# Swapped spectrum halves copied into the dead rows of k in a long convolution fused with an FFN

## The chip, the core and the metric

The kernel runs on one core of a Trainium2 chip. Its engines work side by side, each through its own list of instructions in order: TensorE (PE) for matrix products and transposes, VectorE (DVE), ScalarE (ACT), GpSimd (POOL), and SyncE (SP), which here only issues DMA transfers. They meet through semaphores. The metric is the device time of one execution in microseconds (us); the table below gives the median of the runs.

## The reference

All inputs are bf16; the sequence has 2048 rows of 640 channels. The same normalized input goes into a gated long convolution and into a feed-forward network, and the two results are multiplied:

```python
xn = _layernorm(A_q, axis=-1)
# A: four-tap shift of k, product with v, causal convolution of length 2048 by FFT, times xn
k_shift = sum over t of k_pad[:, t:t + S, :] * shift_k[:, ks - 1 - t]
kv = k_shift * v
y = irfft(rfft(kv, 2 * S) * rfft(ssm_k, 2 * S))[:, :S] + kv * ssm_D
s = xn * y
# B: two layers, 640 -> 1728 -> 640
g = silu(gelu(xn @ w1 + b1) @ w2 + b2)
return A_q + s * g
```

## The kernel before

Everything is on chip but three scratch arrays in DRAM, scrK, scrU and scrC, through which the rows of a transform are regrouped between its two halves. The transforms are matrix products with matrices of sines (WA, WB for the first half; F2m, I1a, I1b in `mats`; GA, GB for the last half). The FFN runs in four chunks of 512 rows.

The order of the work is written out by hand: PLAN is a list of 906 steps, and a loop at the end calls them one after the other. A step is a kind, a number and, for evictions from PSUM, the engine (`.a` ScalarE, `.d` VectorE). The order of the steps of one engine in PLAN is the order of its queue, SP's and POOL's included. Semaphores are set from the data that steps share. The kinds that matter here:

- `P`, `X`, `A`, `B`, `K`, `V`, `C`: loads of parameters, x, w1, w2, k, v and the filter; `pt`, `pb`: transpose of the parameters and the cast of b1 from PSUM, which every `he` needs; `s`, `ss`, `sm`: the small sine matrices; `w`, `ws`: the large ones; `em`, `ee`: the fourth tap's weights.
- `h0` to `h55` and `he`: first FFN layer (five matmuls each) and its gelu on ScalarE, 14 for a chunk. `g0` to `g31`, `ge`, `gm`: second layer (14 matmuls), silu on ScalarE, product on VectorE. `tt`, `te`: transposes of x for a chunk and their copies out; `ls`, `lv`, `lr`, `ln`: the layer norm.
- `cv0` to `cv63`: the shift of k and the product with v on VectorE, eight steps for each of eight pairs of rows. `kt`, `kc`, `kf`, `ke`, `ks`: transpose of the filter, its copy, first transform, cast, store to scrK. `uf`, `ue`, `us`: the same for u = k_shift * v, to scrU.
- `fl`, `ff`, `fe`: load of a pair from scrK, second transform, cast into the spectrum Khat[:, g] (32 blocks g).
- `ml`: load of a pair of u blocks from scrU, after all sixteen `us`. `mu`: their second transform. `mk`: two DMAs that copy a pair of Khat's blocks with their upper and lower 64 partitions exchanged (the "swap"). `mp`: the complex product of u's block, Khat's block and its swap on VectorE. `mc`, `me`, `ms`: first half of the inverse, cast, store to scrC.
- `yl`, `y`, `yt`, `yo`, `ys`: load from scrC, last half of the inverse, gate, sum with x, store. `ga`, `gs`: the same for the last chunk of rows. `q`: load of x for the sum.

Buffers on the way: PSUM has three large tiles ("big") and two small ones ("ffn") that its pools hand out in turn. Khat has 32 spectrum rows and eight more (NR), which the class Ring hands out as four pairs in turn: first to casts of kf and uf, and then to `mk`. The 19 rows of k, the tile kh, are dead once the last `cv` has read them; another Ring hands them out as nine pairs: first to `ml`, then to `yl`.

```python
    pools["ring"] = Ring(Khat, NG, NR // 2)
    pools["line"] = Ring(kh, 0, (NJ + 3) // 2)
```

So a swap waits until the products of the swap four before it are done, and what stands behind it in SP's queue waits too.

Of the kernel before, what the change touches and what calls it, by code (L numbers as in the profile page):

```python
# [50 lines left out]
uf31 gm11 ge12 uf30 ue30.a ue31.d us15 ff23 fe23.d gm12 uf23 ue23.a us11 gm10 tt14 te14.d uf29 uf28 ue28.d
ue29.a us14 mk0 ml0 ml1 mk1 mk2 mk3 ml2 ml3 ml5 ml4 ff31 fe31.a tt13 te13.a tt10 te10.d it0 ie0.d ff27 fe27.d
ff25 fe25.d g13 ge13 gm13 g14 ge14 gm14 ff29 fe29.d ln14 ff28 fe28.a ff24 fe24.d g15 ge15 gm15 ff21 fe21.a tt11
te11.d ff22 fe22.a mu0 mp0 ff26 fe26.a ml7 h28 he28 mu2 mp2 ml10 ml8 mu1 mp1 mk4 mc0 me0.a h29 he29 ff30 fe30.a
mu3 mp3 mk5 ml12 h30 he30 ml11 mc2 me2.a mu4 mp4 mc1 me1.a ms0 mu5 mp5 mk6 h31 he31 ml6 ff20 fe20.a mc3 me3.a
ms1 ln15 mu6 mp6 mc4 me4.a mu7 mp7 mk7 ml9 h32 he32 mu8 mp8 mc5 me5.a ms2 mc6 me6.a mu11 mp11 mc7 me7.a ms3 mu10
mp10 h33 he33 mu9 mp9 mk8 mk9 mc8 me8.a mc10 me10.a mu12 mp12 mu13 mp13 mk10 mc11 me11.a ms5 ml14 h34 he34 ml15
mc12 me12.a it1 ie1.d mc13 me13.a ms6 mu15 mp15 h35 he35 mu14 mp14 mk11 ml13 mc9 me9.a ms4 mu18 mp18 h36 he36
mc14 me14.a mu17 mp17 h37 he37 mu16 mp16 mk12 mc15 me15.a mu20 mp20 h38 he38 mu19 mp19 mk13 mc18 me18.a h39 he39
mu21 mp21 mk14 mc16 me16.a tt17 mc19 me19.a ms9 mc17 me17.a ms8 mu23 mp23 mc20 me20.a mu22 mp22 mk15 h40 he40  # L60
# [14 lines left out]
def kernel(  # L75
# [31 lines left out]
    ps_ffn = ctx.enter_context(tc.tile_pool(name="ps_ffn", bufs=2, space=bass.MemoryType.PSUM))  # L107
    ps_big = ctx.enter_context(tc.tile_pool(name="ps_big", bufs=3, space=bass.MemoryType.PSUM))
# [21 lines left out]
    def big(name):  # L130
        return ps_big.tile([P, 2, 512], F32, tag="big", name=name)
# [9 lines left out]
    Khat = wts.tile([P, NG + NR, D], BF16, name="Khat")  # L141
# [20 lines left out]
    kh = ep.tile([P, NJ + 3, D], BF16, name="kh")  # L162
# [141 lines left out]
    def w_exp_matmuls(j):  # L304
        ps = big("psw")
# [4 lines left out]
        return ps  # L310
# [12 lines left out]
    def big_of(key, bf=False):  # L323
        return take(key, ps_big, [P, 1024] if bf else [P, 2, 512], BF16 if bf else F32, "big")

    def ffn_of(key, bf=False):
        return take(key, ps_ffn, [P, 1024] if bf else [P, 512], BF16 if bf else F32, "ffn")

    def row_of(key):
        return take(key, ep, [P, D], BF16, "row", NROW)  # L330

    def pair_of(key):
        return take(key, ep, [P, 2, D], BF16, "pair", NPAIR)

    def quad_of(key):
        return take(key, ep, [P, CH, D], BF16, "quad", 2)
# [46 lines left out]
    def ffn1_out(i):  # L383
        ft = i % FT
        M = min(P, F - ft * P)
        nc.scalar.activation(out=hT[0:M, ft, :], in_=live["h", i][0:M, :], func=ACT.Gelu_apprx_tanh,  # L386
                             bias=b1_f[0:M, ft:ft + 1], scale=1.0)
# [14 lines left out]
    def ffn2_silu(i):  # L402
        sl = take(("sl", i), ffnp, [P, HALF], BF16, "sl", 2)
        nc.scalar.activation(out=sl[:], in_=live["g", i][:, 0:HALF], func=ACT.Silu)  # L404
# [305 lines left out]
```

## Time and profile before

| what | us |
|---|---|
| three runs: lowest, median, highest | 231.13, 231.67, 232.67 |
| the profiled execution, its own time | 232.81 |
| its span (first to last instruction) | 231.0 |
| mean granted TensorE clock in it | 0.984 |

In the lines below, a group of instructions is given as line, engine, operation, output and inputs by the program's names with buffer numbers left out (so kh, Khat or uc), count, then busy time and mean duration in ns. In a timeline the first number is the start in us from the start of the span, the second the length; in brackets stands how long the engine had been idle, and what ended that. "SPq" rows are issues of DMAs by SyncE. A matmul's record is 0.16 longer than the pace of such matmuls, since neighbours overlap. "DMA to landing" is from the issue to the arrival.

What follows shows where each engine is in the program:

| stretch of the span | work |
|---|---|
| 0 to 16 | loads, layer norm of the first chunk, taps |
| 16 to 57 | first chunk of the FFN, filter's first transform, `cv` on VectorE |
| 57 to 119 | second chunk, first transforms of filter and u, second of the filter |
| 119 to 172 | third chunk's `h`, `mu`, `mp`, `mc` |
| 172 to 231 | rest of the third chunk, last inverse, fourth chunk, outputs |

### The profile page before, as it was taken

The page shows a single profiled execution, that of the slowest core. Times are in us where ns is not written, and L with a number is a line of the kernel's source. Part 1 is how long each engine was busy: PE and PEld are TensorE (multiplying, and loading weights), DVE is VectorE, ACT ScalarE, POOL GpSimd, SP SyncE. Part 2 cuts the span into 40 slices and gives each one's busy share as a digit, 9 for nine tenths or more (in the row PEclk, how much of TensorE's full clock was granted, in tenths as well). Part 3 has the DMA queues.
Part 4 walks back from the last instruction along what each step waited for, and adds up shares of the span by engine and source line. Part 5 has one row for each costly group of instructions (what it writes and reads, how often), then busy time and mean ns, then how long its engine had stood idle before and what let it go on. Part 6 is the DMA issues. An engine that isn't in the chain of part 4 may idle for free.

```text
span 231.0 us, 3921 instructions
## 1 busy us (share of the span) xinstructions
PE 211.6 (92%) x1420; PEld 131.7 (57%) x1420; DVE 184.1 (80%) x315; ACT 149.6 (65%) x232; POOL 43.1 (19%) x75
## 2 busy tenths in 40 slices
PE   7859999899999899979999965999999999999993
PEld 4524456677555556646765532556677765457772
DVE  7799999889989999999779885699998115444892
ACT  3934687998988999898468742567782244562111
POOL 8100020042232344120200220212222000100010
PEclk9988999999999999999999997999999999999999
DMA  7999995654844479599779999877943695379323
GB/s 219 349 380 355 409 413 206 191 209 174 305 191 188 179 236 381 176 309 337 266 215 294 303 353 295 257 231 188 270 156 131 207 340 200 150 218 367 124 89 114
DMA packets 25209, 57.61 MB, mean 249 GB/s; under 512 B 2854, under 2 KB 14055, under 8 KB 25190
## 3 DMA queue, kind: packets, MB, share of 16 engines
q1 hardware_dynamic: 20726, 39.66, 52.6%
q0 software_dynamic: 4320, 17.70, 20.5%
q8 instruction: 11, 0.18, 0.3%
q14 instruction: 8, 0.07, 0.1%
q10 hardware_dynamic: 144, 0.01, 0.0%
HBM read 33.76 MB, written 18.35 MB: 226 GB/s over the span
## 4 chain that ended last, share of the span: by engine, by line
PE 65%; ACT 12%; DMA 9%; DVE 8%; issue 3%; SPq 1%; DVEq 0%; ACTq 0%
PE g L399 22%; PE h L380 21%; ACT Khat L135 6%; DMA kh<-scrU 6%; PE uf L340 3%; PE mc L537 3%; DMA Khat<-Khat 3%; PE mc L538 2%; PE mu L340 2%; PE kf L340 2%; PE ff L340 2%; PE y L556 2%; PE y L557 2%; DMA skp<-in_A_shift_k_dram 1%; ACT sl L404 1%
## 5 line engine op out<-in xcount | busy, mean ns | idle before, releaser
L380 PE MATMUL h<-xnT,w_sb 128*128 128x512 bf16 x280 | 68.4, 390 | 1.5 <-ACT hT L386 1.2
L399 PE MATMUL g<-w_sb,hT 128*128 128x320 bf16 x448 | 63.7, 299 | 0.6 <-ACT sl L404 0.6
L386 ACT ACTIVATE hT<-h,b_f 128x512 bf16<-128x512 f32 (+1 forms) x56 | 38.3, 690 | 27.3 <-PE h L380 24.2
L399 PEld LDWEIGHTS <-hT 128*128 128x128 bf16 x448 | 43.8, 98 | 18.1 <-issue 0.8
L529 DVE TENSOR_TENSOR p<-mu,Khat 128x1280 bf16<-128x1280 f32 x32 | 45.8, 1484 | 5.4 <-PE mu L340 3.7
L380 PEld LDWEIGHTS <-w_sb 128*128 128x128 bf16 x280 | 27.9, 100 | 31.3 <-issue 4.6
L404 ACT ACTIVATE sl<-g 128x320 bf16<-128x320 f32 x32 | 13.9, 439 | 36.1 <-PE g L399 32.5
L135 ACT CAST c<-mc 128x640 bf16<-128x640 f32 x29 | 19.9, 692 | 8.6 <-PE mc L538 7.9
L544 POOL DMA_DIRECT2D scrC<-c x16 | 11.5, 718 | 56.0 <-ACT c L135 51.8
L409 DVE TENSOR_TENSOR xn<-xn,sl 128x320 bf16<-128x320 bf16 x32 | 10.1, 322 | 14.0 <-ACT sl L404 13.8
L472 DVE TENSOR_TENSOR uc<-uc,kvtmp 128x1280 bf16<-128x1280 bf16 x24 | 19.8, 824 | 0.7
L476 DVE TENSOR_TENSOR kvtmp<-kh,w_exp 128x1280 bf16<-128x1280 bf16 x24 | 19.7, 820 | 0.5
L340 PEld LDWEIGHTS <-mats 128*128 128x128 bf16 x128 | 12.1, 97 | 13.8 <-issue 4.9
L537 PE MATMUL mc<-p,mats 128*128 128x320 bf16 x64 | 18.6, 305 | 1.2 <-DVE p L529 0.7
L538 PE MATMUL mc<-p,mats 128*128 128x320 bf16 x64 | 18.5, 304 | 0.0
L563 DVE TENSOR_TENSOR t<-y,xn 128x640 bf16<-128x640 f32 x12 | 9.8, 820 | 10.4 <-PE y L557 10.3
L135 ACT CAST Khat<-uf 128x640 bf16<-128x640 f32 x26 | 17.0, 697 | 0.4 <-PE uf L340 0.4
L340 PE MATMUL mu<-kh,mats 128*128 128x320 bf16 x64 | 13.5, 300 | 3.7 <-DMA kh<-scrU 2.5
L135 ACT CAST Khat<-ff 128x640 bf16<-128x640 f32 x24 | 15.5, 699 | 0.5 <-PE ff L340 0.4
L135 ACT CAST Khat<-kf 128x640 bf16<-128x640 f32 x22 | 15.1, 711 | 0.3 <-PE kf L340 0.2
L440 POOL DMA_DIRECT2D scrK<-Khat x16 | 8.9, 554 | 31.2 <-ACT Khat L135 16.6
L340 PE MATMUL ff<-kin,mats 128*128 128x320 bf16 x64 | 12.3, 298 | 1.4 <-ACT Khat L135 1.3
(111 smaller groups left out, 269.4 us busy)
## 6 DMA issues: line engine op xcount, KB each, us to landing
scrK<-Khat POOLq DMA_DIRECT2D x16, 320.0 KB, 2.6
scrU<-Khat POOLq DMA_DIRECT2D x16, 320.0 KB, 4.2
kin<-scrK SPq DMA_DIRECT2D x16, 320.0 KB, 4.6
Khat<-Khat SPq DMA_DIRECT2D x32, 160.0 KB, 4.2
kh<-scrU SPq DMA_DIRECT2D x16, 320.0 KB, 5.4
scrC<-c POOLq DMA_DIRECT2D x16, 320.0 KB, 3.9
kh<-scrC SPq DMA_DIRECT2D x16, 320.0 KB, 6.2
kh<-in_A_k_dram SPq DMA_DIRECT2D x4, 640.0 KB, 6.1
```

What stands on the lines that cost most here:

```text
L135: return nc.scalar.copy(out=out_ap, in_=in_ap)
L340: nc.tensor.matmul(out=ps[:, h, 0:HALF], lhsT=lhsT, rhs=rhs[:, h * HALF:(h + 1) * HALF], start=start, stop=stop)
L380: nc.tensor.matmul(out=ps[:, :], lhsT=w1_sb[:, t, ft * P:(ft + 1) * P], rhs=xnT[:, t, :], start=(t == 0), stop=(t == DT - 1))
L386: nc.scalar.activation(out=hT[0:M, ft, :], in_=live["h", i][0:M, :], func=ACT.Gelu_apprx_tanh, bias=b1_f[0:M, ft:ft + 1], scale=1.0)
L399: nc.tensor.matmul(out=ps[:, 0:HALF], lhsT=hT[0:M, ft, q * P:(q + 1) * P], rhs=w2_sb[0:M, ft, hs], start=(ft == 0), stop=(ft == FT - 1))
L404: nc.scalar.activation(out=sl[:], in_=live["g", i][:, 0:HALF], func=ACT.Silu)
L472: nc.vector.tensor_tensor(out=uc[:], in0=uc[:], in1=kvtmp[:], op=ALU.add)
L476: nc.vector.tensor_tensor(out=(kvtmp if s else uc)[:], in0=kh[:, r0:r0 + KC, :], in1=w_exp[:, j:j + 1, :].to_broadcast([P, KC, D]), op=ALU ...
L529: nc.vector.tensor_tensor(out=p[:].rearrange("p k (h c) -> p k h c", h=2), in0=live["mu", g][:, None, :, 0:HALF].to_broadcast([P, 2, 2, HA ...
L537: nc.tensor.matmul(out=psC[:, h, 0:HALF], lhsT=I1a, rhs=p[:, 0, hs], start=True, stop=False)
L538: nc.tensor.matmul(out=psC[:, h, 0:HALF], lhsT=I1b, rhs=p[:, 1, hs], start=False, stop=True)
L544: nc.gpsimd.dma_start(out=pair_view(scrC)[g2], in_=live["c", g2][:])
```

## The change

The swaps now go where k was, nine pairs, and the u loads go into the four pairs behind the spectrum. For this kh is no tile of its own but 19 more rows of Khat, so that one access pattern reaches from a spectrum block to its swap. In place of the pools' turns, a class Slots keeps a list of free buffers for PSUM and for the work tiles: the one that was given back first is taken first, and each is given back after a stated number of uses. And PLAN is written anew, all of it.

```diff
+    class Slots:
+        def __init__(self, views):
+            self.free, self.held = list(views), {}
+        def take(self, key, uses):
+            self.held[key] = [self.free.pop(0), uses]
+            return self.held[key][0]
+        def use(self, key):
+            t = self.held[key]
+            t[1] -= 1
+            if t[1] == 0:
+                self.free.append(t[0])
+                del self.held[key]
+            return t[0]
+    big = Slots(big_tiles[2:] + big_tiles[:2])
+    ffn = Slots(ffn_tiles)
...
-    Khat = wts.tile([P, NG + NR, D], BF16, name="Khat")
+    Khat = wts.tile([P, NG + NR + NJ + 3, D], BF16, name="Khat")
...
-    kh = ep.tile([P, NJ + 3, D], BF16, name="kh")
+    kh = Khat[:, NG + NR:NG + NR + NJ + 3, :]
...
     def uin_load(g2):
-        nc.sync.dma_start(out=take(("uin", g2), pools["line"], None, None, None), in_=pair_view(scrU)[g2])
+        nc.sync.dma_start(out=take(("uin", g2), pools["ring"], None, None, None), in_=pair_view(scrU)[g2])
...
     def swap_load(g2):
-        ks = take(("ks", g2), pools["ring"], None, None, "ks")
+        swap_row[g2] = NG + NR + pools["line"].next_row()
+        ks = take(("ks", g2), pools["line"], None, None, "ks")
...
     def product(g):
-        p = pair_of(("p", g))
-        swap = NG + g % NR
+        p = pair.take(("p", g), 1)
+        swap = swap_row[g // 2] + g % 2
...
 PLAN = """
-em K0 sp s A0 h0 h1 P2 ee.a A1 P1 P0 pt pb he0 he1 h2 he2 h3 he3 h4 he4 h5 he5 h6 he6 h7 he7 h8 he8 h9 he9 h10
+P2 X1 P1 P0 A0 pt h0 h1 pb he0 he1 h2 h3 he2 he3 A1 h4 he4 h5 he5 h6 h7 he6 he7 h8 he8 h9 he9 h10 he10 h11 he11
```

The number of steps is the same. Of the casts and copies that leave PSUM, VectorE does 38 and ScalarE 126 in the new list, where it was 44 and 120. One load of an activation table is gone: `ss` stood between the gelus of chunk one and the silus, and stands among the silus now.

SP's queue, where the swaps (`Khat<-Khat`), the last loads from scrK (`kin`) and the loads from scrU (`kh<-scrU`) are issued. Before:

```order
L480 DMA kin_1407<-scrK 128x2x640
L480 DMA kin_1417<-scrK 128x2x640
L521 DMA Khat<-Khat 64x1280 x2
L516 DMA kh<-scrU 128x2x640 x2
L521 DMA Khat<-Khat 64x1280 x6
L516 DMA kh<-scrU 128x2x640 x7
L521 DMA Khat<-Khat 64x1280 x4
L516 DMA kh<-scrU 128x2x640 x2
```

Now, where the loads from scrK go to `pair` buffers and those from scrU to Khat's rows:

```order
L537 DMA Khat<-Khat 64x1280 x2
L492 DMA pair_114<-scrK 128x2x640
L492 DMA pair_118<-scrK 128x2x640
L537 DMA Khat<-Khat 64x1280 x2
L492 DMA pair_115<-scrK 128x2x640
L492 DMA pair_117<-scrK 128x2x640
L492 DMA pair_116<-scrK 128x2x640
L492 DMA pair_113<-scrK 128x2x640
L492 DMA pair_115<-scrK 128x2x640
L537 DMA Khat<-Khat 64x1280 x2
L529 DMA Khat<-scrU 128x2x640 x2
L537 DMA Khat<-Khat 64x1280 x2
```

Two pairs of swaps moved ahead of loads from scrK and three ahead of the first load from scrU, where it was one; of the loads from scrU two now follow where seven stood in a row.

VectorE behind the first chunk's copies, before: the end of the list of small operations of `s`, then b1's cast (`b_f`) and the first convolution step.

```order
L293 TENSOR_SCALAR Khat<-GA 128x384
L294 TENSOR_SCALAR Khat<-Khat 128x384
L512 CAST b_f<-pt_296 128x14
L513 COPY dD_sb<-pt_296 128x5
L476 TENSOR_TENSOR uc_388<-kh,w_exp 128x1280
```

Now, from the copies of the first chunk on:

```order
L158 COPY xnT<-f_79 128x512
L158 COPY xnT<-b_75 128x512
L525 CAST b_f<-b_77 128x14
L526 COPY dD_sb<-b_77 128x5
L359 BN_STATS st_338<-xn 128x6 x2
```

b1's cast moved from behind `s` to right behind the copies, and statistics of the second chunk follow it; `s` comes after those.

More of the change, by code (lines that the diff above doesn't have):

```diff
@@ L51 @@
[L51 to L60, printed above, removed]
@@ new lines @@
+fe10.d g15 fl12 ff17 gm13 fe13.a ge15 gm14 fe11.d ff28 fe17.a fe28.d ff12 fe12.a mk2 tt13 ff22 ff23 fe22.a
+te13.d fe23.d ff21 fe21.a ln14 tt12 te12.d ff27 fe27.a ff24 fe24.a gm15 it0 ie0.d ml0 ml1 mk3 ff20 ml5 ml3
+fe20.a mk4 mk5 mk6 ff31 fe31.a ff26 fe26.d ff30 fe30.a mu0 ff25 fe25.a mu1 mp0 mp1 h28 he28 mc0 me0.a mu3 ml2
+h29 mu2 mc1 mp3 mu6 mp2 me1.a ms0 ml6 mp6 h30 he30 mk7 mk8 mk9 mc2 me2.a mc3 me3.a mu10 mc6 me6.a ln12 mu4 mu11
+he29 mp10 mu5 h31 mp4 mp5 he31 ml4 mc10 me10.a h32 he32 mu7 mk10 mp11 mc4 me4.a ms1 mp7 ml7 ml8 h33 he33 mu8 mu9
@@ new lines @@
+mc7 me7.a h34 he34 mp8 mp9 mc8 me8.a mc11 me11.a ms3 mu12 mc5 me5.a mp12 mu13 h35 mu17 mc9 me9.a h36 he36 mp13
+mu14 ml9 mp17 ml11 it2 ie2.a mu15 ml10 mk11 mk12 mk13 mk14 mk15 mp14 mp15 h37 he37 mc12 me12.a mc13 me13.a he35
+ms5 ms2 it1 ie1.d it3 ie3.a mu18 h38 he38 mp18 ms4 mu16 ml12 mp16 mc14 me14.a mu19 ml14 h39 he39 mc16 me16.a
+mu20 mp19 mp20 h40 he40 ms6 mc15 me15.a mu23 mc18 me18.a ms7 mp23 tt17 mc19 me19.a mc17 me17.a mu22 mp22 ml13
+h41 he41 mu21 mc20 me20.a mp21 mu24 mp24 g16 ge16 mu25 mp25 mu26 mc21 me21.a mp26 te17.a g17 ge17 gm17 mc22
@@ L321, in take @@
         return live[key]
[L323 to L336, printed above, removed]
+    work = {name: Slots([ep.tile([P] + ([n] if n > 1 else []) + [D], BF16, name="%s%d" % (name, i)) for i in range(bufs)])
+            for name, n, bufs in (("row", 1, NROW), ("pair", 2, NPAIR), ("quad", CH, 2))}
+    row, pair, quad = work["row"], work["pair"], work["quad"]
     def mm2(ps, lhsT, rhs, start=True, stop=True):
@@ L454, in __init__, with next_row @@
             self.rows, self.first, self.pairs, self.n = rows, first, pairs, 0
+        def next_row(self):
+            return self.first + 2 * (self.n % self.pairs)
         def tile(self, *_, **__):
-            r0 = self.first + 2 * (self.n % self.pairs)
+            r0 = self.next_row()
             self.n += 1
@@ L479, in kin_load @@
     def kin_load(g2):
-        nc.sync.dma_start(out=pair_of(("kin", g2))[:], in_=pair_view(scrK)[g2])
+        nc.sync.dma_start(out=pair.take(("kin", g2), 2)[:], in_=pair_view(scrK)[g2])
     def k_f2(g):
-        mm2(big_of(("ff", g)), F2m, live["kin", g // 2][:, g % 2, :])
+        mm2(big.take(("ff", g), 1), F2m, pair.use(("kin", g // 2))[:, g % 2, :])
     def k_f2_out(g, eng):
-        cast(eng, Khat[:, g, :], live["ff", g])
+        cast(eng, Khat[:, g, :], big.use(("ff", g)))
     def i2_tr(i):
-        tp = big_of(("it", i), True)
+        tp = bf_view(big.take(("it", i), 1))
         for q in range(8):
@@ L540, in inv1_out @@
     def inv1_out(g, eng):
-        cast(eng, pair_of(("c", g // 2))[:, g % 2, :], live["mc", g])
+        c = pair.held["c", g // 2][0] if g % 2 else pair.take(("c", g // 2), 1)
+        cast(eng, c[:, g % 2, :], big.use(("mc", g)))
     def c_store(g2):
-        nc.gpsimd.dma_start(out=pair_view(scrC)[g2], in_=live["c", g2][:])
+        nc.gpsimd.dma_start(out=pair_view(scrC)[g2], in_=pair.use(("c", g2))[:])
     def xq_load(c):
-        nc.sync.dma_start(out=quad_of(("xq", c))[:], in_=x_v[:, c * CH:(c + 1) * CH, :])
+        nc.sync.dma_start(out=quad.take(("q", c), 2 * CH if c == NCH - 1 else CH)[:], in_=x_v[:, c * CH:(c + 1) * CH, :])
     def cab_load(n2):
@@ L623, in prologue @@
         warm(WARM0)
-        psw = [w_exp_matmuls(j) for j in range(3)]
+        psw = big_tiles
+        for j in range(3):
+            w_exp_matmuls(j, psw[j])
         for j in (0, 1):
```

136 lines of the change are left out of this document (68 added, 68 removed).

## The prediction

> **What bounds the kernel now.** I read the page's totals first, then the busy time of each engine in seven stretches that I cut where the work changes: 16.05 is where the first layer of the FFN restarts, 57.09 and 84.45 are starts of its second chunk's layers, 119.06 is the first `mu` (the second transform of u), 172.49 the end of the last `mu`.
>
> ```profile
> span 231.0 us, 3921 instructions
> PE 211.6 (92%) x1420; PEld 131.7 (57%) x1420; DVE 184.1 (80%) x315; ACT 149.6 (65%) x232; POOL 43.1 (19%) x75
> 0.00:16.05 16.05, 10.70 (x82) 6.24 (x83) 13.10 (x55) 9.28 (x15) 6.08 (x18) 0.99 0.92 313
> 16.05:57.09 41.04, 39.33 (x269) 24.77 (x269) 37.68 (x68) 32.19 (x47) 5.39 (x8) 0.96 0.78 287
> 57.09:84.45 27.36, 26.35 (x170) 15.44 (x168) 26.09 (x49) 25.64 (x42) 8.35 (x16) 1.00 0.56 205
> 84.45:119.06 34.61, 31.97 (x234) 21.44 (x232) 30.91 (x54) 27.26 (x48) 8.52 (x13) 1.00 0.83 284
> 119.06:172.49 53.43, 48.50 (x312) 28.75 (x311) 46.18 (x39) 35.68 (x53) 8.64 (x13) 0.97 0.89 266
> 172.49:208.55 36.06, 36.06 (x227) 21.88 (x225) 16.24 (x28) 16.07 (x25) 4.49 (x7) 1.00 0.60 204
> 208.55:231.00 22.45, 18.66 (x138) 13.18 (x135) 13.90 (x30) 3.51 (x9) 1.63 (x3) 0.99 0.45 171
> ```
>
> The columns are length, then PE, PEld, DVE, ACT, POOL busy, granted clock, DMA share, GB/s. Behind 172.49 TensorE has no gap at all: there only the amount of matmul work left counts. Ahead of 119.06 VectorE is as full as TensorE (37.68 of 41.04, 26.09 of 27.36), and the last convolution step, which the last uf transforms wait for, is VectorE's. Between the two stands a hole, shown on PE, DVE and the SP queue:
>
> ```profile
> 135.08 0.43 PE L340 MATMUL mu<-kh,mats 128*128 128x320 bf16 x2 [0.81 <-DVE p L529]
> 135.35 1.24 PE L380 MATMUL h<-xnT,w_sb 128*128 128x512 bf16 x5
> 138.18 0.30 PE L537 MATMUL mc<-p,mats 128*128 128x320 bf16 x1 [0.69 <-DVE p L529]
> 141.42 0.78 PE L340 MATMUL mu<-kh,mats 128*128 128x320 bf16 x4 [2.54 <-DMA kh<-scrU]
> 143.06 2.34 PE L380 MATMUL h<-xnT,w_sb 128*128 128x512 bf16 x5
> 133.53 1.49 DVE L529 TENSOR_TENSOR p<-mu,Khat 128x1280 bf16<-128x1280 f32 x1 [1.50 <-DMA Khat<-Khat]
> 131.02 2.16 SPq L521 DMA_DIRECT2D Khat<-Khat  x2
> 133.27 0.54 SPq L516 DMA_DIRECT2D kh<-scrU  x1
> ```
>
> The swap copy `mk6` needs a pair of the ring of four that a product still reads, so it stands in the SP queue until 133, and the u load behind it (issued at 133.27) is what `mu12` waits for at 141.42. After the hole the same five matmuls take 2.34 instead of 1.24.
>
> **Prologue.** The parameter loads now precede w1, and the b1 cast precedes the two dozen small VectorE operations of `s`.
>
> ```profile
> 11.86 1.67 PE L380 MATMUL h<-xnT,w_sb 128*128 128x512 bf16 x7 [0.30 <-ACT xnT L135]
> 14.66 0.17 PE L508 MATMUL pt<-ident,prm 19*128 19x19 bf16 x1 [1.13 <-DMA prm<-in_B_b_dram]
> 16.05 14.58 PE L380 MATMUL h<-xnT,w_sb 128*128 128x512 bf16 x60 [1.22 <-ACT hT L386]
> 9.94 1.09 DVE L136 COPY xnT<-tpx 128x512 bf16<-128x512 bf16 x3 [0.32 <-PE tpx L657]
> ```
>
> h2 can start behind h1, at about 13.4, not 16.05: 2.65. The 60 matmuls take 14.58, and 12 times 1.08 (five at full pace, 1.24 less the 0.16 by which records overlap) is 12.96: 1.6 more was slow clock. Ten tap matmuls (0.5) move behind h13. PE gains 3.75. I carry none of it to the end: VectorE starts its list at 9.94 and 11.0 in both kernels, and it is the fuller one. The gain is cover for the other direction. Should the parameters land late behind x1 (640 KB now ahead of w1), the same 3.75 is lost again, at no cost either.
>
> **VectorE ahead of the last convolution step (cv63).** Counting steps in the two tables up to cv63: casts of kf on VectorE 10 to 4, of ff 3 to 1, of uf 3 to 5, copies of kt 7 to 9, of tt 1 to 3, normalizations 10 to 8, gate products 10 to 12.
>
> ```profile
> L136 DVE CAST Khat<-kf 128x640 bf16<-128x640 f32 x10 | 8.1, 821 | 1.4 <-PE kf L340 1.4
> L136 DVE COPY kT<-kt 128x640 bf16<-128x640 bf16 x7 | 3.4, 489 | 0.9 <-PE kt L424 0.4 <-ACT Khat L135 0.3
> L364 DVE TENSOR_SCALAR xn<-xn,mv,rs 128x640 bf16<-128x640 bf16 x12 | 5.0, 441 | 0.0
> L409 DVE TENSOR_TENSOR xn<-xn,sl 128x320 bf16<-128x320 bf16 x32 | 10.1, 322 | 14.0 <-ACT sl L404 13.8
> L136 DVE COPY xnT<-tt 128x512 bf16<-128x512 bf16 x7 | 2.8, 419 | 0.0
> 105.89 0.82 DVE L470 TENSOR_TENSOR uc<-uc,vc 128x1280 bf16<-128x1280 bf16 x1
> L135 ACT CAST Khat<-kf 128x640 bf16<-128x640 f32 x22 | 15.1, 711 | 0.3 <-PE kf L340 0.2
> L298 ACT ACT_TABLE_LOAD x1 | 1.3, 1283 | 0.0
> ```
>
> That is six casts less net (6 + 2 - 2) at 0.82, two copies at 0.49 and two at 0.42 more, two normalizations at 0.44 less, two products at 0.32 more: -4.92 + 0.98 + 0.84 - 0.88 + 0.64 = -3.3, or -3.2 with the overlap of neighbours. cv63 ends at 106.71 now, so at 103.5. ScalarE takes six more kf casts (4.2) and drops one table load (1.28), since `ss` now runs with the table of silu. It has 8.9 idle in the stretch to 57.09 but 1.7 in the next; without that cover the 2.9 show (a rival below).
>
> **From cv63 to the first `mu`.**
>
> ```profile
> 111.54 0.54 POOL L450 DMA_DIRECT2D scrU<-Khat  x1 [0.74 <-ACT Khat L135]
> 116.13 0.88 SPq L516 DMA_DIRECT2D kh<-scrU  x2
> 119.06 0.43 PE L340 MATMUL mu<-kh,mats 128*128 128x320 bf16 x2
> 176.73 11.43 PE g L399 x84
> ```
>
> Now it takes 12.35 (106.71 to 119.06). After: four uf pairs with their casts, about 2.5, then store to load to `mu` 7.5 (111.54 to 119.06) makes 10.0; TensorE's list behind the last uf is two g (1.90 each, from six in 11.43), fifteen ff at 0.27, and 0.9 of transposes, 8.75, after 1.6 of uf: 10.35, with some waits for casts 10.7. I take 10.7: `mu0` at 114.2, 4.85 earlier. TensorE alone could be there at 119.06 - 3.75 - 5.4 (its idle time from 16.05 to 119.06) + 0.5 = 110.4, so VectorE decides. Three swap copies now run ahead of the u loads: 960 KB, 3.4 at the 284 GB/s of that stretch, where the share was 0.83, so 5.9 was free. Bounds 0 and 1.1 (one pair of 320 KB ahead of the last store); I take 0, since two of the three stand ahead of the last five uf's in the table. The Trainium skill (DMA: Bandwidth & Descriptors, Issuing engines are not separate DMA queues) speaks against this move: transfers from all queues share the same 16 engines, so copies from SP would slow the stores from POOL; by it the sum would be up to 1.1 higher.
>
> **From `mu0` to the last `mu`.** 53.43 now. Out go the waits 0.81 + 0.69 + 2.54 and the slow matmuls behind them (1.10 for h, 0.5 for six short ones): 5.6. Two more g's are done here (+3.8), two ff fewer (-0.5). Freeing products of their ring has a price: u loads fall from nine pairs to four. Twelve of them wait until a pair's second `mu` is done, and the table leaves TensorE this much work before the same pair is read: 4.3 for ml13, 4.9 for ml4, 7.0, 7.0 and 7.1 for ml2, ml9 and ml10, over 8.5 for the rest.
>
> ```profile
> L516 SPq DMA_DIRECT2D kh<-scrU x16: 365/476/1270, 116.1 to 151.5; - x16
> DMA to landing us min/median/max: 3.4/5.4/8.5
> ```
>
> 0.48 and 5.4 are 5.9: ml13 is 1.6 late and ml4 1.0. VectorE's queued products cover part; bounds 0 and 2.6, I take 1.0. Sum: -5.6 + 3.8 - 0.5 + 1.0 = -1.3. The skill's fit for one transfer (same page, Anatomy of one DMA) is 2.0 us plus size at 436 GB/s, an estimate of 2.75 for 320 KB; by it none is late and the sum is 1.0 lower. The trace has 5.4, and that is used.
>
> **Behind the last `mu`.** 58.5 now without a gap; two g's fewer remain: -3.8. The first y waits for every c store and then for its load:
>
> ```profile
> 178.81 0.72 POOL L544 DMA_DIRECT2D scrC<-c  x1 [0.51 <-DVE c L136]
> 181.80 4.86 SPq L550 DMA_DIRECT2D kh<-scrC  x9
> DMA to landing us min/median/max: 2.8/6.2/7.4
> ```
>
> Cast 0.8, 3.0 from store to first load (178.81 to 181.80), 0.4 of issue and 2.8 to 6.2 of landing make 7.0 to 10.4. The cover in the new table is four g and two h behind the last mc, 9.8; bounds 0 and 0.6, I take 0.
>
> **Sum.** -4.85 - 1.3 - 3.8 = -9.95. The profiled execution took 232.81 with a span of 231.0; the median of the runs shown, 231.67, lies 1.14 below it. 232.81 - 9.95 - 1.14 = 221.7.
>
> **Rivals.** (a) The ring of four turns on the SP queue: with swaps ahead of it each u load lands at the upper end, 8.5. Then 9.0 against the work above: 4.7, 4.1, 2.0, 2.0, 1.9 and small ones, 15.4 instead of 1.0: 236, slower than before. At 7.8 it takes back the whole gain, from 8.2 it is slower by over 1%. For it: the stretch had DMA share 0.89. Against: swaps come earlier, and half of the landings were under 5.4. (b) The swaps do not get ahead, because they stand in SP's order behind kin and u loads; the hole stays: +4.6, 226.3. (c) ScalarE, full from 57 to 84, hands its 2.9 on: 224.6. (d) VectorE is not the bound after all and TensorE's 110.4 to 111 stands, no load late: -4.2, 217.5. A single wait of some 3 us on cv63 would also cost slow matmuls (1.6, as after 141.42): 223.3, inside the range. By the skill (TensorE: Matmul & The Clock Gate, What's actually happening) a window of about 3.4 us must be idle; here 2.54 with two short waits before it was enough.
>
> **Chances.** Forecast 0.50 (219.5 to 224), d 0.17, c 0.14, b 0.13, a 0.06. The range 216.5 to 228 leaves out a and the ends. 1% is about what a measurement can tell here. b, c, d and the forecast are all faster by over 1% (under 229.4), 0.94; I take 0.06 off for mixtures of b and c that end near the time before: faster 0.88, same 0.06, slower 0.06.
>
> **What would show it.** VectorE's cv63 ends near 103.5, the first `mu` starts near 114 and the last ends near 166; no PE wait over 1.5 for a u load; no slow matmul behind 16; h2 starts before 14; one table load less. Wrong if VectorE is idle for several us ahead of cv63, or if the waits for u loads sum to over 5.

## The result, and the profile after

The new kernel takes 225.25 us (median of four runs, 222.02 to 228.25) where the kernel before takes 231.65 beside it: a ratio of 0.963, with a 95% interval from 0.953 to 0.974 (two of the four runs, 226.08 and 228.25, were disturbed; such runs, of either kernel, count in the medians here and in no ratio). A second set of four runs gave 224.68 and 0.965 (0.956 to 0.974). Faster, as forecast. Of 231.65 the ratio leaves 223.1, 1.4 above the forecast of 221.7; the medians are 3 to 3.5 above it, just outside the 219.5 to 224 that were given to the forecast itself and inside the whole range of 216.5 to 228.

The profiled execution took 224.42 with a span of 222.3. First its totals, then the busy time of each engine in the same stretches as before, cut at the first `mu` and within the last one (length, then PE, PEld, DVE, ACT, POOL busy, granted clock, DMA share, GB/s):

```profile
span 222.3 us, 3924 instructions
PE 206.1 (93%) x1406; PEld 129.9 (58%) x1420; DVE 177.7 (80%) x309; ACT 151.0 (68%) x237; POOL 42.4 (19%) x75
0.00:16.00 16.00, 12.39 (x84) 6.45 (x86) 13.16 (x48) 10.18 (x16) 6.07 (x18) 1.00 0.90 287
16.00:55.00 39.00, 36.63 (x276) 24.32 (x277) 36.12 (x70) 33.20 (x50) 5.84 (x9) 1.00 0.88 319
55.00:81.00 26.00, 25.59 (x161) 15.11 (x163) 25.34 (x53) 25.35 (x43) 9.36 (x16) 1.00 0.64 222
81.00:114.19 33.19, 31.62 (x232) 21.25 (x230) 28.88 (x51) 26.88 (x46) 6.48 (x11) 1.00 0.95 310
114.19:166.64 52.45, 48.82 (x329) 30.35 (x335) 46.19 (x39) 35.30 (x53) 9.28 (x13) 1.00 0.88 266
166.64:200.00 33.36, 33.20 (x204) 19.98 (x205) 15.84 (x25) 15.41 (x25) 3.24 (x5) 1.00 0.66 224
200.00:222.30 22.30, 17.84 (x130) 12.47 (x128) 12.13 (x28) 4.70 (x9) 2.14 (x4) 1.00 0.42 139
```

By stages the forecast met the trace closely. The first `mu` starts at 114.19 (forecast 114.2), the last one ends at 166.8 (166.3), and 55.5 follow (54.7). The clock is full throughout in this profile; before, it was 0.96 to 0.97 in two stretches. But the first of the three agrees by two errors that cancel. The start of TensorE's list, and then the rows around the last convolution step, of VectorE, TensorE, POOL and the SP queue:

```profile
11.87 14.62 PE L389 MATMUL f<-xnT,w_sb 128*128 128x512 bf16 x65 [0.41 <-ACT xnT L157]
28.20 3.03 PE L408 MATMUL f<-w_sb,hT 128*128 128x320 bf16 x21 [1.15 <-DMA w_sb<-in_B_w_dram]
100.60 0.82 DVE L482 TENSOR_TENSOR pair<-pair,quad 128x1280 bf16<-128x1280 bf16 x1
102.09 0.43 PE L349 MATMUL b<-pair,WA 128*128 128x320 bf16 x2
103.33 0.43 PE L349 MATMUL b<-pair,WB 128*128 128x320 bf16 x2
105.65 0.54 POOL L459 DMA_DIRECT2D scrU<-Khat  x1 [0.54 <-issue]
109.89 1.17 SPq L529 DMA_DIRECT2D Khat<-scrU  x2
114.19 0.45 PE L349 MATMUL b<-Khat,mats 128*128 128x320 bf16 x2 [0.38 <-DMA Khat<-scrU]
```

TensorE runs without a stop from `h2` to the fourth tap (`em`) and reaches the second layer of the FFN at 28.20, where it waits for w2. The row at 100.60 is cv63; it ends at 101.42, not at 103.5 as forecast. Four `uf` steps need it, the last ones, `uf28` to `uf31`: the rows at 102.09 and 103.33 are the first and the last of them. The first starts 0.67 after cv63, and the profile shows no wait for VectorE in front of any of the four. So here the last `uf` came when TensorE's own list had reached it, not because VectorE was late; but VectorE had only 0.67 to spare. From its last `uf` (103.33) through store, load and first `mu` another 10.9 pass.

In the `mu` stage the waits have changed hands. These are TensorE's waits between 112 and 156 but for one of 0.2 (total, times, longest):

```profile
PE b L349 <- DMA Khat<-scrU: 3.4, 4, 1.2
```

Of waits for swaps VectorE has 0.3 left, and TensorE none behind them; four waits for u loads took their place. And at the end TensorE loses 0.65 in a chain that begins with an output store. The rows of VectorE, ScalarE and TensorE:

```profile
207.01 0.49 DVE L584 TENSOR_TENSOR w_exp<-row,quad 128x640 bf16<-128x640 bf16 x1 [3.20 <-DMA out_dram<-w_exp]
209.80 0.33 DVE L418 TENSOR_TENSOR xn<-xn,sl 128x320 bf16<-128x320 bf16 x1
210.22 0.44 ACT L413 ACTIVATE sl<-f 128x320 bf16<-128x320 f32 x1 [4.58 <-DVE xn L418]
210.71 7.78 PE L408 MATMUL f<-w_sb,hT 128*128 128x320 bf16 x56 [0.65 <-ACT sl L413]
```

VectorE stands 3.20 for the buffer that a store still reads, so its product with a silu (209.80) comes late; that product frees the buffer of the next silu (210.22), and this silu the PSUM tile that TensorE waits for.

### The profile page after: what moved, and what is told of

It is laid out like the page before. It is cut to its first block, busy times and chain, and to the rows that moved or that the text cites. A ratio compares the mean times of both kernels' runs of the same rounds, so it can differ in the third digit from the quotient of the medians.

```text
span 222.3 us, 3924 instructions
## 1 busy us (share of the span) xinstructions
PE 206.1 (93%) x1406; PEld 129.9 (58%) x1420; DVE 177.7 (80%) x309; ACT 151.0 (68%) x237; POOL 42.4 (19%) x75
## 4 chain that ended last, share of the span: by engine, by line
PE 68%; DMA 19%; ACT 6%; DVE 3%; issue 2%; SPq 1%; DVEq 0%; ACTq 0%
PE f L408 25%; PE f L389 17%; PE b L349 13%; DMA w_sb<-in_B_w_dram 9%; DMA Khat<-scrU 7%; ACT Khat L157 5%; PE b L553 3%; PE b L554 3%; DMA xn<-in_A_q_dram 3%; PE b L433 2%; PE b L574 2%; PE b L573 2%; ACT sl L413 1%; PE f L380 1%; DVE pair L545 1%
## 5 line engine op out<-in xcount | busy, mean ns | idle before, releaser
L408 PE MATMUL f<-w_sb,hT 128*128 128x320 bf16 x448 | 64.5, 299 | 1.9 <-DMA w_sb<-in_B_w_dram 1.1
L389 PE MATMUL f<-xnT,w_sb 128*128 128x512 bf16 x266 | 64.3, 379 | 1.0 <-ACT xnT L157 0.4
L395 ACT ACTIVATE hT<-f,b_f 128x512 bf16<-128x512 f32 (+1 forms) x56 | 38.2, 696 | 24.0 <-PE f L389 23.2
L157 ACT CAST Khat<-b 128x640 bf16<-128x640 f32 x78 | 50.7, 709 | 3.0 <-PE b L349 2.7
L545 DVE TENSOR_TENSOR pair<-b,Khat 128x1280 bf16<-128x1280 f32 x32 | 46.1, 1486 | 5.2 <-PE b L349 4.2
L157 ACT CAST pair<-b 128x640 bf16<-128x640 f32 x31 | 20.9, 693 | 9.7 <-PE b L554 9.1
L488 DVE TENSOR_TENSOR kvtmp<-Khat,w_exp 128x1280 bf16<-128x1280 bf16 x24 | 19.6, 818 | 0.6 <-ACT w_exp L157 0.4
L484 DVE TENSOR_TENSOR pair<-pair,kvtmp 128x1280 bf16<-128x1280 bf16 x24 | 19.7, 821 | 0.4
L553 PE MATMUL b<-pair,mats 128*128 128x320 bf16 x64 | 18.1, 299 | 0.1
L554 PE MATMUL b<-pair,mats 128*128 128x320 bf16 x64 | 18.1, 299 | 0.0
L158 DVE CAST Khat<-b 128x640 bf16<-128x640 f32 x18 | 14.8, 820 | 3.7 <-PE b L349 2.6
L349 PE MATMUL b<-pair,mats 128*128 128x320 bf16 x64 | 12.3, 298 | 1.0 <-ACT Khat L157 0.5
```

What stands on the lines that cost most here:

```text
L157: return nc.scalar.copy(out=out_ap, in_=in_ap)
L158: return nc.vector.tensor_copy(out=out_ap, in_=in_ap)
L349: nc.tensor.matmul(out=ps[:, h, 0:HALF], lhsT=lhsT, rhs=rhs[:, h * HALF:(h + 1) * HALF], start=start, stop=stop)
L389: nc.tensor.matmul(out=ps[:, :], lhsT=w1_sb[:, t, ft * P:(ft + 1) * P], rhs=xnT[:, t, :], start=(t == 0), stop=(t == DT - 1))
L395: nc.scalar.activation(out=hT[0:M, ft, :], in_=ffn.use(("h", i))[0:M, :], func=ACT.Gelu_apprx_tanh, bias=b1_f[0:M, ft:ft + 1], scale=1.0)
L408: nc.tensor.matmul(out=ps[:, 0:HALF], lhsT=hT[0:M, ft, q * P:(q + 1) * P], rhs=w2_sb[0:M, ft, hs], start=(ft == 0), stop=(ft == FT - 1))
```

## Experiments

Kernels that are compared here ran beside the kernel before; the table gives median and ratio (with its interval), and from each profile: when `g0` starts, cv63 ends, the last `uf` starts, the first `mu` starts. Differences in time below are of these medians where no ratio is named.

| kernel | median us | ratio to before | g0 | cv63 ends | last uf | first mu |
|---|---|---|---|---|---|---|
| before | 231.67 | 1 | 30.47 | 106.71 | 109.56 | 119.06 |
| after | 225.25 | 0.963 (0.953 to 0.974) | 28.20 | 101.42 | 103.33 | 114.19 |
| again | 224.68 | 0.965 (0.956 to 0.974) | 27.28 | 100.43 | 102.42 | 115.54 |
| cv_less | 225.48 | 0.973 (0.966 to 0.980) | 27.27 | 99.83 | 102.41 | 113.50 |
| cv_more | 226.69 | 0.979 (0.972 to 0.985) | 27.51 | 103.18 | 104.80 | 115.92 |
| s_first | 229.91 | 0.995 (0.989 to 1.000) | 31.14 | 104.69 | 106.78 | 118.01 |
| b_params | 239.27 | 1.028 (1.021 to 1.034) | 27.43 | 112.85 | 115.74 | 125.24 |
| rings_back | 232.81 | 1.002 (0.997 to 1.007) | 27.51 | 100.25 | 102.65 | 113.25 |
| ring6 | 230.44 | 0.994 (0.989 to 1.000) | 27.76 | 100.34 | 102.92 | 113.90 |
| ring6m | 229.90 | 0.984 (0.976 to 0.993) | 27.22 | 100.86 | 102.65 | 113.71 |
| s_first_em | 227.57 | 0.979 (0.972 to 0.986) | 29.23 | 101.75 | 104.32 | 115.59 |
| b_params_em | 232.48 | 1.001 (0.996 to 1.006) | 26.30 | 106.56 | 109.64 | 119.25 |
| ring6q | 225.89 | 0.962 (0.953 to 0.971) | 27.47 | 100.46 | 102.94 | 114.32 |
| ring6qh | 225.82 | 0.972 (0.965 to 0.979) | 27.32 | 100.07 | 102.66 | 115.22 |

### again: the same program once more

> The changed kernel once more, beside the next three on one chip. Both theories: first mu at 114.2 and last mu ending at 166.6 in its profile (within 0.5), span near 222, time between 221.5 and 225; it shows how far two profiles of the same program differ.

Median 224.68, last `uf` at 102.42, 0.9 earlier than in the first profile, because w2 was there in time. Still the first `mu` came 1.35 later, at 115.54, after a wait of 2.0 for its load: two profiles of one program differ by over 1 at this point, through the time that DMAs take, and this wait is longer than the 1.5 that the prediction allowed for a u load:

```profile
115.54 0.72 PE L350 MATMUL b<-Khat,mats 128*128 128x320 bf16 x2 [2.04 <-DMA Khat<-scrU]
```

So the first `mu` is a poor mark for small effects; the start of the last `uf` is the better one.

### cv_less and cv_more: VectorE's load ahead of cv63

```diff
-cv51 cv52 uf21
+cv51 uf21
...
-cv54 ue23.d
+ue23.d
...
-cv58 cv59 cv60 g10
+cv58 cv59 g10
...
-lv3 cv62 cv63
+lv3 cv63
```

> Leaves out four of the additions of the shifted k (cv52, cv54, cv60, cv62; 4 x 0.82 = 3.3 of VectorE, all behind 81 us). Theory of the prediction (VectorE's work ahead of cv63 sets the first mu): cv63 ends 3.3 earlier, at 98.1, the first mu comes at 110.9, the time falls by 3.3. Rival (TensorE's own list sets it: it has no gap from 53.6 to 110.8, and uf30 started 1.4 behind the end of cv63): cv63 earlier by 3.3 all the same, but uf30 within 0.3 of 102.8, the first mu within 0.5 of 114.2, no gain in time (under 0.5).

The edit of cv_more, in four places:

```diff
-cv51 cv52
+cv51 cv51 cv52
```

> Four products of the shifted k (cv51, cv53, cv59, cv61) are computed twice, 3.3 more of VectorE behind 81 us, nothing else. Theory of the prediction: the first mu 3.3 later, at 117.5, time +3.3. Rival (TensorE): the 1.4 of slack between cv63 and uf30 is used up first: cv63 ends near 104.7, uf30 at 104.7, the first mu 1.9 later at 116.1, time +1.9, or less if the swaps and u loads use the time.

The last convolution step and the last `uf`, of again, then of cv_less:

```profile
99.60 0.83 DVE L483 TENSOR_TENSOR pair<-pair,quad 128x1280 bf16<-128x1280 bf16 x1
102.42 0.43 PE L350 MATMUL b<-pair,WB 128*128 128x320 bf16 x2
```

```profile
95.18 0.33 DVE L418 TENSOR_TENSOR xn<-xn,sl 128x320 bf16<-128x320 bf16 x1 [1.16 <-ACT sl L413]
96.31 0.82 DVE L158 CAST Khat<-b 128x640 bf16<-128x640 f32 x1 [0.80 <-DMA scrU<-Khat]
99.01 0.82 DVE L482 TENSOR_TENSOR pair<-pair,quad 128x1280 bf16<-128x1280 bf16 x1
102.41 0.43 PE L349 MATMUL b<-pair,WB 128*128 128x320 bf16 x2
```

With 3.3 less to do, VectorE ended only 0.6 earlier: it now waited for others, 1.16 for a silu and 0.80 for a store in the rows above, and 1.0 for ScalarE and 0.9 for TensorE ahead of them (the expectation that cv63 would move by 3.3 was wrong). The last `uf` did not move at all, and nothing was gained. With 3.3 more, cv63 ended 2.75 later, the last `uf` 2.4 later, and the time rose by 2.0 (0.979 against 0.965; the two intervals overlap a little). Three rows of TensorE in cv_more hold these 2.4:

```profile
87.39 0.43 PE L350 MATMUL b<-pair,WA 128*128 128x320 bf16 x2 [1.33 <-DVE Khat L159]
103.23 0.45 PE L350 MATMUL b<-pair,WA 128*128 128x320 bf16 x2 [0.51 <-DVE pair L483]
104.53 0.43 PE L350 MATMUL b<-pair,WA 128*128 128x320 bf16 x2 [0.58 <-DVE Khat L159]
```

The middle one is `uf28`, which waits for cv63; the other two wait for casts of VectorE that free a PSUM tile. The rival was near in size (1.9), but its account, 1.4 of slack and then the rest, is not what happened: most of the loss came through casts. So TensorE's list decides in the new kernel as it stands, VectorE has 0.7 to spare at cv63 (in again it ends at 100.43, and `uf28` starts at 101.18) and less at its casts, and more work on either engine costs time. The delay of the last `uf` reaches the end of the stage: from it to the start of the last `mu` 65.1 pass in again, 65.4 in cv_less and 65.0 in cv_more (63.2 in the first profile).

### s_first and s_first_em: the old start in the new kernel

```diff
-P2 X1 P1 P0 A0 pt h0 h1 pb he0 he1 h2 h3 he2 he3 A1 h4
+X1 A0 sp s h0 h1 P2 A1 P1 P0 pt pb he0 he1 h2 h3 he2 he3 h4
...
-K2 K3 sp s lv1
+K2 K3 lv1
```

> The start of the old order in the new kernel: the small VectorE operations of s ahead of the b1 cast, the parameter loads between w1's halves. Both: h2 starts near 15.5 to 16 instead of 13.17, h13 ends 2.4 to 3.75 later than 26.12. Theory of the prediction (none of the prologue's gain is carried): first mu within 0.5 of 114.2, time within 0.5. Rival (TensorE's list is the bound): the wait for w2 at g0 (1.39) covers a part, the rest is passed on: first mu 1.0 to 2.4 later, time +1.0 to +2.4.

It cost 5.2, more than either theory had, but it held both engines: VectorE waited 4.4 for the fourth tap's weights, since `em` stands behind h13. So it could not tell them apart, and the next one puts `em` and `ee` at the start:

```diff
-X1 A0 sp s h0 h1 P2 A1 P1 P0 pt pb he0 he1
+X1 em A0 sp s h0 h1 P2 ee.a A1 P1 P0 pt pb he0 he1
...
-lr1 em ee.a cv3
+lr1 cv3
```

> s_first delayed VectorE too (4.4 of waiting for the fourth tap's weights, behind h13). Here the fourth tap (em, ee) stands at the start as in the old kernel, s ahead of the b1 cast, parameters between w1's halves: TensorE's start is as late as the old one (h2 near 15.5, h13 ending near 30), VectorE's list is not held. Theory of the prediction (VectorE decides, the prologue's gain is not carried): first mu and time within 0.8 of the new kernel. Rival (TensorE decides in the new kernel, VectorE with 1.4 of slack): first mu 2.5 to 4 later, time +2.5 to +4.

Of s_first_em the restart of `h`, cv63, and the first and the last `uf` that need it:

```profile
16.28 13.11 PE L389 MATMUL f<-xnT,w_sb 128*128 128x512 bf16 x59 [1.34 <-ACT hT L395]
100.92 0.83 DVE L482 TENSOR_TENSOR pair<-pair,quad 128x1280 bf16<-128x1280 bf16 x1
103.08 0.43 PE L349 MATMUL b<-pair,WA 128*128 128x320 bf16 x2
104.32 0.43 PE L349 MATMUL b<-pair,WB 128*128 128x320 bf16 x2
```

TensorE starts `g0` 1.95 later than in again (29.23; no slow clock this time, so less than in s_first), and its last `uf` comes 1.9 later. VectorE is 1.3 later too (cv63 ends at 101.75; in the profile of after at 101.42), but this comes from TensorE, for whose transposes it waited 1.7 on the way (0.4 in again), and it isn't what the `uf` steps wait for: the first of them starts 1.33 after cv63, where it was 0.75 in again. The first `mu`, at 115.59, is no later than again's 115.54, but 1.3 to 2.3 later than in the five other kernels of the table in which TensorE has the same steps up to it (113.25 to 114.32: cv_less, rings_back, ring6, ring6m, ring6q). The last `mu` starts 65.5 after the last `uf`, as in the others. The time rose by 2.9, to 0.979 against 0.965. The prologue's gain is carried in the new kernel.

### b_params and b_params_em: the new start in the old kernel

```diff
-em K0 sp s A0 h0 h1 P2 ee.a A1 P1 P0 pt pb he0 he1
+P2 P1 P0 A0 pt h0 h1 pb he0 he1 A1
...
-he13 K3
+he13 K0 sp s em ee.a K3
```

> The old kernel with the new start alone: parameter loads and the b1 cast ahead, s, em and the first k load behind h13. Both: h2 starts near 13.2 to 13.8 instead of 16.05 and h13 ends 3.5 to 4.5 earlier than 30.6. Theory of the prediction (VectorE's list is the fuller one in the old kernel, so nothing is carried): cv63 ends within 0.8 of 106.71, first mu within 0.8 of 119.06, time within 0.8 of the kernel before. Rival (TensorE's list carries it, as undoing it in the new kernel cost 5.2 and moved the first mu by 2.5 to 3.8): first mu at 115 to 116, time 3 to 4.5 shorter.

One row of VectorE explains the loss of 6.6. It is a product with the fourth tap's weights, which `em`, now behind h13, makes:

```profile
28.39 0.82 DVE L476 TENSOR_TENSOR kvtmp<-kh,w_exp 128x1280 bf16<-128x1280 bf16 x1 [6.54 <-ACT w_exp L135]
```

TensorE was 3.0 earlier at `g0`, VectorE was held for 6.54, and the first `mu` came 6.2 later. Neither theory had put a number to that. TensorE was held in its turn (6.54 at 42.59, for a silu behind a product of VectorE), so in the old kernel this delay of VectorE passed to the end one to one, and what TensorE had gained was lost with it. The next kernel leaves `em` and K0 first:

```diff
-em K0 sp s A0 h0 h1 P2 ee.a A1 P1 P0 pt pb he0 he1
+em K0 P2 P1 P0 A0 pt h0 h1 ee.a pb sp s he0 he1 A1
```

> The old kernel with the parameter loads and the b1 cast ahead of s, everything else of its start where it was (em and K0 first): h2 near 13.5, h13 ending 3 to 4 earlier, VectorE not held for the fourth tap as it was in b_params (6.5). Theory of the prediction (VectorE decides in the old kernel): time within 0.8 of the kernel before. Rival: 3 to 4 shorter.

```profile
11.38 15.08 PE L380 MATMUL h<-xnT,w_sb 128*128 128x512 bf16 x68 [0.16 <-issue]
26.30 3.97 PE L399 MATMUL g<-w_sb,hT 128*128 128x320 bf16 x28
105.73 0.83 DVE L470 TENSOR_TENSOR uc<-uc,vc 128x1280 bf16<-128x1280 bf16 x1
```

TensorE reaches `g0` 4.2 earlier, cv63 and the first `mu` stay (106.56 and 119.25), and so does the time (1.001, 0.996 to 1.006). In the old kernel nothing of it is carried, as the prediction held.

### rings_back: the swaps in the ring of four again

```diff
-        swap_row[g2] = NG + NR + pools["line"].next_row()
-        ks = take(("ks", g2), pools["line"], None, None, "ks")
+        swap_row[g2] = pools["ring"].next_row()
+        ks = take(("ks", g2), pools["ring"], None, None, "ks")
...
-ie0.d ml0 ml1 mk3 ff20 ml5 ml3 fe20.a mk4 mk5 mk6 ff31
+ie0.d mk0 ml0 ml1 mk1 mk2 mk3 ml3 ml5 ff20 fe20.a ml2 ml4 ml6 ml7 ml8 ff31
...
-mp4 mp5 he31
+mp4 mp5 mk6 ml9 ml11 he31
```

Two of the places are shown; PLAN moves the other `mk` to later places too, and most `ml` to earlier ones.

> The new kernel with swaps in the ring of four and u loads in the nine pairs again; mk and ml moved only as far as the data then ask (mk0 behind it0, each mk from the fifth on behind the products that free its pair). Theory of the prediction: the hole comes back (5.6 of waits and slow clock) and the u ring's 1.0 goes: time +4.6, near 229, PE waiting over 2 at once in the mu stage. Rival (the exchange only puts waits for u loads in the place of waits for swaps): time within 1.5 of the new kernel, the stage from the first to the last mu within 1.5 of 52.

```profile
120.00 14.74 SPq L538 DMA_DIRECT2D Khat<-Khat  x6
129.28 5.68 DVE L546 TENSOR_TENSOR pair<-b,Khat 128x1280 bf16<-128x1280 f32 x4 [5.99 <-DMA Khat<-Khat]
130.82 0.69 PE L350 MATMUL b<-Khat,mats 128*128 128x320 bf16 x2 [3.79 <-DVE pair L546]
113.25:173.93 60.68, 51.76 (x329) 31.54 (x335) 46.56 (x39) 35.71 (x53) 9.31 (x13) 0.94 0.83 247
```

The hole is back, in the same stage: swaps occupy the SP queue from 120 to 134.7, a product waits 6.0 for one, TensorE 3.8 for the product, and the stage's mean clock falls to 0.94. The stage from the first to the last `mu` takes 60.7 instead of 52.5, the time rises by 8.1 to that of the kernel before. The theory had the mechanism and 4.6 of it. Another part is a wait of 2.33 for a u load (at 120.69), behind which five matmuls of an `h` take 2.34 as well. That the new order, made for early swaps, suits late ones badly is likely, but was not tested apart. Nor did any run exchange the rings alone in the old order, or bring in the class Slots alone, so what each part of the change is worth by itself stays open.

### ring6, ring6m, ring6q, ring6qh: more pairs for u loads

```diff
+    pools["uring"] = Pairs([Khat[:, NG + 2 * i:NG + 2 * i + 2, :] for i in range(NR // 2)]
+                           + [w_exp[:, 2 * i:2 * i + 2, :] for i in range(2)])
```

> The new kernel with six pairs for u loads in place of four (two pairs of w_exp, dead behind cv63, join the ring), the order as it was. Theory U (pairs held too long cost what the trace shows as waits for u loads in the mu stage, 3.9 behind the first mu in the profile of after): ml2 and ml6 are no longer held, 1.4 to 2 less. Rival S (they stand in SP's queue behind swap copies, and land in 5 to 6 whatever frees their pair): under 0.7 less.

ring6m has this too, and in PLAN, with ml4 and ml7 moved as told (mk7 to mk9 stood behind he30 already):

```diff
-ml0 ml1 mk3 ff20 ml5 ml3 fe20.a mk4 mk5 mk6 ff31
+ml0 ml1 ml3 mk3 ml2 ml5 mk5 ml6 ff20 fe20.a mk4 mk6 ff31
```

> As ring6, and the u loads moved ahead of the swaps that are not needed yet: ml3, ml2, ml5 and ml6 between ml1 and mk4, ml4 behind mu1, ml7 behind mu2, mk7 to mk9 behind he30. Theory U and S both: no wait over 0.7 for a u load behind the first two, stage from first to last mu 3 shorter, time -2 to -3.5 (near 221). Rival D (the transfers are the limit in that stage, DMA share 0.9 and more): loads that are issued earlier land later, the swaps with them, time within 0.7.

All theories missed: 230.44 and 229.90, 5 to 6 slower. The SP queue, a store, ScalarE and TensorE of ring6m, then the SP queue, the same store and ScalarE of again:

```profile
149.36 0.94 SPq L575 DMA_DIRECT2D quad<-in_A_q_dram  x2
151.54 0.72 POOL L572 DMA_DIRECT2D scrC<-pair  x1 [6.46 <-ACT pair L158]
159.74 0.69 ACT L158 CAST pair<-b 128x640 bf16<-128x640 f32 x1 [4.87 <-DMA scrC<-pair]
160.49 1.22 PE L350 MATMUL b<-Khat,mats 128*128 128x320 bf16 x4 [3.34 <-ACT pair L158]
162.57 3.67 PE L409 MATMUL f<-w_sb,hT 128*128 128x320 bf16 x13
```

```profile
155.24 1.79 SPq L565 DMA_DIRECT2D quad<-in_A_q_dram  x2
151.92 0.72 POOL L562 DMA_DIRECT2D scrC<-pair  x1 [6.43 <-ACT pair L158]
155.57 0.69 ACT L158 CAST pair<-b 128x640 bf16<-128x640 f32 x1 [0.33 <-DMA scrC<-pair]
```

In again the last u load waits for its pair and holds what stands behind it in SP's queue, two loads of x (1.3 MB), back to 155.24. With six pairs they go out at 149.36, ahead of three stores to scrC. The store issued by 152.26 frees its buffer at 159.74, 7.5 later; in again that took 2.9 (152.64 to 155.57). ScalarE waits for the buffer, TensorE for ScalarE, and the next 13 matmuls of `g` take 3.67 at a slow clock (0.50 from 160 to 165). ring6, whose order is untouched, has the same wait (3.37 at 161.82), and one of 2.70 for a u load. The Trainium skill (DMA: Bandwidth & Descriptors, Issuing engines are not separate DMA queues) says that transfers of all queues interleave on the same 16 engines; the store that takes 7.5 instead of 2.9 agrees with that. ring6q tests it by moving only these two loads:

```diff
-me27.a q1 q0 mp30
+me27.a mp30
...
-yl0 yl1 yl6 yl7 yl5 yl2
+yl0 yl1 q0 yl6 yl7 yl5 q1 yl2
```

> ring6m with the loads of x for the sum (q0, q1; 1.3 MB) moved behind the first loads of the last stage (yl1, yl5). Theory Q (the ring of four held ml15 in SP's queue to 154.8 and with it q0 and q1; freed, they start at 150, ahead of three stores to scrC, which then land after 7.4 instead of 4.2, and ScalarE waits 4.9 for the pair): the 5.2 that ring6m lost come back, no PE wait over 1 behind g16, time 223 to 225, or 1 to 2 under the new kernel if the loads that are no longer late count. Rival (six pairs cost by themselves, or the wait has another cause): stays near 229.

225.89: 4.0 of the 5.2 come back, and the ratio, 0.962, is that of the new kernel. ScalarE then waits for no store between 145 and 170, and the clock is 1.00 from 160 to 165. So the collision is shown. What is not there is a gain: two more pairs and earlier u loads are worth nothing that these runs can measure. The last kernel moves an `h` ahead of the first `mu`:

```diff
-fe30.a mu0 ff25 fe25.a mu1
+fe30.a ff25 fe25.a h28 he28 mu0 mu1
```

> ring6q with ff25 and h28 ahead of mu0: TensorE has 1.35 more work while the last u store and the first u load are under way (it waited 0.7 to 2.3 there). Theory: 0.5 to 1.3 shorter than ring6q. Rival: h28 is missing behind mu1 as cover for the first product, the wait moves to mc0, within 0.3.

```profile
PE b L350 <- DVE pair L556: 1.7, 2, 1.5
PE b L564 <- DVE pair L556: 1.5, 2, 1.3
```

These are the two largest of its waits from 112 to 176, for a free large PSUM tile and for a product, 3.2 together; it has none for a u load. What was taken from the waits for loads came back as waits for products; the time stays, 225.82. No version here beats the new kernel.

## Why the prediction was right, point by point

**Prologue: the step that failed.** "I carry none of it to the end" holds in the old kernel (b_params_em) and not in the new one (s_first_em: 1.95 at `g0`, 1.9 at the last `uf`, 2.9 in the time). The reason given, that VectorE "is the fuller one", was a fact of the old profile, and the change removes it in the same stroke, by making VectorE's list to cv63 5.3 shorter. "TensorE alone could be there at 110.4" took away all of TensorE's 5.4 of idle time; 4.35 remain in the three stretches from 16 to 114.19 (39.00 less 36.63, 26.00 less 25.59, 33.19 less 31.62). With them the same sum gives 114.75, near the 114.19 that was measured. That TensorE's list was the bound rests on cv_less and s_first_em, not on this sum.

**VectorE ahead of cv63: mis-sized, 5.3 instead of 3.2.** The count of steps was right. What it left out stands in three rows of the kernel before:

```profile
26.52 0.83 DVE L476 TENSOR_TENSOR kvtmp<-kh,w_exp 128x1280 bf16<-128x1280 bf16 x1
27.38 0.82 DVE L472 TENSOR_TENSOR uc<-uc,kvtmp 128x1280 bf16<-128x1280 bf16 x1
28.12 0.82 DVE L476 TENSOR_TENSOR uc<-kh,w_exp 128x1280 bf16<-128x1280 bf16 x1
```

A step that shares its operand with the one in front of it starts 0.86 after it (26.52 to 27.38), another one 0.74 after (27.38 to 28.12). Up to cv63 the old table has 37 such neighbours and the new one 20: 17 times 0.12 is 2.0, and 3.3 and 2.0 make the 5.3. This closes the sum, but no kernel tested it alone. Waits are not the cause: VectorE's from 9.9 to cv63 add up to 3.3 before and 3.9 after.

**First `mu`: the right number by two errors, which is luck.** cv63 came 2.1 earlier than forecast, and the way from it to the first `mu` was 12.8 instead of 10.7. Of these 2.1, 0.7 is that `uf28` had to wait for TensorE's turn; the rest lies behind the last `uf`, where 10.6 pass to the first `mu` (103.60 to 114.19) and the forecast had 9.1 (8.75 and 0.35 of waits). There TensorE's list ran out 0.38 before the u load landed, and the way from the last store to the first `mu` took 8.5 (105.65 to 114.19) instead of 7.5. Both engines had gained, VectorE more than counted and TensorE less than hoped; rival (d) was right that VectorE is not the bound, and wrong that TensorE would be at 110.4.

**`mu` stage: the mechanism right, two sizes not.** Forecast 52.1, measured 52.6. The hole is gone because the swaps stand in nine pairs (rings_back), rival (b) is out. The waits for u loads were mis-sized: behind the first `mu` they are 3.0 (3.4 less the 0.38 in front of it) and not 1.0. In the two tables of stretches TensorE's idle time in the stage falls by 1.3 (4.93 to 3.63), where the terms of the forecast give 3.0 (4.04 out, 1.0 in), and its busy time rises by 0.3 (48.50 to 48.82), where they give 1.7 (3.8 less 0.5 less 1.6). The two errors cancel; why the busy time rose so little no run shows. Taking the waits for u loads away (ring6qh) gained nothing. Rival (a) did not come: the u loads landed in 3.5 to 6.2, half of them under 5.0. The fit of the Trainium skill that the prediction put beside its sum (DMA: Bandwidth & Descriptors, Anatomy of one DMA) is given there for transfers that GpSimd issues, and SyncE issues these. Rival (c) did not come either: TensorE's waits for ScalarE between 53 and 114 add up to 0.9, where it needed 2.9.

**Behind the last `mu`.** Forecast 54.7, measured 55.5; the 0.65 that began with an output store is most of the difference, and the first `y` did not wait. **From span to time:** forecast span 221.05, measured 222.3. This 1.25 is close to the 1.4 by which the ratio misses. Of the 3.55 by which the median was missed another 0.3 lies outside the span (2.1 of 224.42, 1.8 of 232.81 before), and 2.0 is where the profiled runs lay: that of before 1.14 above its median, that of after 0.83 below. Runs of one kernel spread over 2 to 3% (222.02 to 228.25 after; 229.2 to 234.8 for before beside the first group of experiments), so a forecast from one profile is hard to judge more closely than that.

## What to carry to other kernels

When two engines are both nearly full, a gain on one can be worth nothing until the other gains too (cv_less and b_params_em here), so judge it against the profile that the whole change leaves, and never credit an engine with all its idle time. A wait that holds a queue also holds what stands behind it: before you remove one, list the transfers that will start earlier and what they will meet. A forecast that agrees in total can still be wrong in its steps; an experiment that delays one engine tells, if you also check in its profile whether the other engine was left alone.

## What the runs showed of the hardware

- On VectorE a bf16 product of 128x1280 started 0.74 behind an independent neighbour and 0.86 behind one with which it shares the operand that one of them writes, though each has a duration of 0.82. The Trainium skill (VectorE: DVE Perf Modes, Two Vector instructions with no wait between them) tells an instruction that starts only when every earlier one has finished from one that starts sooner. The two paces agree with there being two kinds. The section's rule goes by the partitions at which operands start, and these are the same in all these rows; what sets them apart here is the shared operand.
- The length of a wait alone did not decide whether the clock fell. Behind the wait of 2.04 in again it did, and behind one of 2.67 in s_first_em it stayed full; so did waits of up to 1.2 in the profile of after. The stretch around the wait of again, then the longer wait of s_first_em and the stretch behind it (length, busy times, then the granted clock, 0.86 and 1.00):

```profile
113.00:125.00 12.00, 9.92 (x51) 5.29 (x50) 8.41 (x8) 6.79 (x10) 0.73 (x1) 0.86 0.97 248
123.32 0.45 PE L349 MATMUL b<-Khat,mats 128*128 128x320 bf16 x2 [2.67 <-DMA Khat<-scrU]
123.00:128.00 5.00, 3.73 (x22) 2.08 (x23) 3.34 (x3) 2.92 (x5) 0.73 (x1) 1.00 1.05 287
```
